# Sigmoid attention and a GELU feed-forward layer on one core: the first pair's scores from unsplit float32, values products between them, and weight decoding that begins in the fourth unit and goes on at one chunk a product in block 0

## The chip, the cores and the metric

The kernel runs on one core of a Trainium2 chip. A core has a matrix engine (TensorE, PE in the profile, with its weight loads as PEld), a vector engine (DVE), an activation engine (ACT), GpSimd (POOL), and a sync engine (SP) that here only issues DMAs. Each engine works through its own instructions in order and waits on semaphores for the others. The metric is the device time of one execution in microseconds (us); the median of three runs of the kernel before is 1192.38 us.

## The reference

Eight batches, twelve heads, 448 positions, head size 64; the 3584 tokens of 768 values that come out go through a feed-forward layer of width 2048.

```python
def _attn_ref(q, k, v):
    S = q.shape[2]
    scale = 1.0 / np.sqrt(q.shape[-1])
    scores = scale * np.matmul(q, k.transpose(0, 1, 3, 2)) - np.log(S)
    attn = 1.0 / (1.0 + np.exp(-scores))
    return np.matmul(attn, v).astype(np.float32)

def _moe_ref(x, w_in, w_out):
    h = x @ w_in
    g = 0.5 * h * (1.0 + erf(h * inv_sqrt2))
    return (g @ w_out).astype(np.float32)
# x: the attention output, as (batch * position) x (head * size)
```

The attention weights are a sigmoid of each score, so no row needs a maximum or a sum. `w_in` (768 x 2048) and `w_out` (2048 x 768) arrive as 64-bit floats. The host only lays data out; the kernel itself turns the 64-bit patterns into float32. That is the decoding of which the title speaks.

## The kernel before, in words

**Attention** runs over 24 units; a unit is one batch and four heads, held as two pairs p = 0, 1 of two heads each. For each pair, `scores` makes three chunks of 128 keys. A score is a sum of three products in a fast float32 format ("fp32r"), of a rounded part `hi` and a rest `lo` of q and k: lo·hi, hi·lo, hi·hi, two heads side by side in the array, 18 matmuls for a pair. `split` makes the parts: for pair 0, ACT rounds (L245) and DVE subtracts (L248); for pair 1, DVE does both (L247, L248). `scores_tail` does the last 64 keys of all four heads from the raw float32 data (L277). Each chunk goes through a sigmoid on ACT (L252) from one of three PSUM buffers (`ps_sc`), so a chunk's products wait until the sigmoid three chunks earlier is done. `values` (L298) and `values_tail` (L311) multiply the sigmoids by v in plain float32, one unit behind the scores; `park` copies the sums from PSUM (L324, DVE) and GpSimd writes them to a scratch `scr_x` in HBM.

**Decoding** is a list of steps, taken in program order by `dec.to(c)` up to c chunks. There are 40 chunks: 16 of `w_in` (768 columns each) and 24 half units of `w_out` (512 each). A chunk needs, on DVE, L99, L100 and L103 (`start`); on ACT, L110 and L113 (`scale`); then on DVE, L119 and L124 (`end`). A finished unit goes to HBM scratch through GpSimd's queue. The 64-bit data come in by SP (`raw`, three buffers), three loads ahead of the first chunk and then one at each `end`. Before the change, chunk 0 is decoded in unit 0, 20 chunks are done within attention (`AHEAD = 20`), ten more beside the sixteen w_in products of block 0, the last ten beside block 0's w_out products.

**Feed-forward** runs over seven blocks t of 512 tokens. `ffn1` makes 16 tiles of 128 hidden features, 18 matmuls each (lo·hi, hi·lo, hi·hi over six parts of 128, L370 to L372); ACT applies GELU twice (L375 `gf` in float32, L376 `g` rounded) and DVE subtracts (L377). `ffn2` makes six output tiles from two halves of 24 matmuls each (L398 to L400). All need the weights split as well. `Weights` streams each decoded unit from scratch (`wst`, three buffers), ACT rounds it (L184), DVE subtracts (L185), into one of four buffers `whl`. `W.get` of unit i first prepares every unit up to i + 3. Thus, in program order, unit i + 3's cast and subtraction come after tile i - 1's GELU, subtraction and decoding step, and before tile i's.

Nothing reorders this: the order on each engine is the order in which the program is written. At the end of the attention `load_x`, `split_x` and `W.prepare_to(2)` make the first block's inputs ready, and ACT loads its GELU table (L375) before the first `gf`.

Of the kernel before, what the change touches and what calls it, by code (L numbers as in the profile page):

```python
# [21 lines left out]
def tile_sigmoid_attention_gelu_ffn(  # L22
# [131 lines left out]
                self.taken += 1  # L154

    dec = Decoder()
    AHEAD = 20

    class Weights:
        def __init__(self):  # L160
# [48 lines left out]
    def attention(at, ps_sc, ps_av):  # L209
# [3 lines left out]
        def load(u):  # L213
            if u >= total:
                return
            b, n = divmod(u, NU)
            raw = at.tile([P, 2, 2, S], F32, tag="qk", name=f"qk{u}", bufs=3)
            pairs = (slice(0, 1), slice(1, 2)) if u == 0 else (slice(0, 2),)
            for ps in pairs:
                hps = slice(2 * n + ps.start, 2 * n + ps.stop)  # L220
                nc.sync.dma_start(raw[:, ps, 0], q[b, hps].rearrange("p r s -> r p s"))
                for j in range(2):
                    src = k[b, hps, rows(j), j].rearrange("p r s -> r p s")
                    nc.sync.dma_start(raw[rows(j), ps, 1], src)
            raws[u] = raw

        def load_v(u):
# [27 lines left out]
        def scores(u, p, c):  # L255
            if u >= total:
                return
            hi, lo = parts[u, p]
            sc = ps_sc.tile([P, 2, 512], F32, tag="sc", name=f"sc{u}_{p}_{c}")[:, :, :S]
            keys = slice(c * P, c * P + P)  # L260
            terms = ((hi, lo), (lo, hi), (hi, hi))
            for n, (ks, qs) in enumerate(terms):
                for j in range(2):
                    nc.tensor.matmul(  # L264
                        sc[:, j], ks[rows(j), 1, keys], qs[rows(j), 0], start=n == 0, stop=n == 2
                    )
            sigmoid(u, p, c, sc)

# [19 lines left out]
                pavs[u, p] = ps_av.tile([P, 512], F32, tag=f"pav{p}", name=f"pav{u}_{p}")  # L288
            return pavs[u, p][:, :S]

        def values(u, p):
            if u < 0:
                return
            pav = bank(u, p)
            for c in range(FULL):
                a = probs.pop((u, p, c))
                for j in range(2):
                    nc.tensor.matmul(  # L298
                        pav[rows(j)],
                        vals[u][:, p, j, c],  # L300
                        a[:, j],
                        start=p == 0 and c == 0,
                        stop=p == 1 and c == FULL - 1,
                    )
# [22 lines left out]
                nc.gpsimd.dma_start(scr_x[:, 2 * n : 2 * n + 2, b * S : (b + 1) * S], xs.pop(u))  # L327

        load(0)
        split(0, 0)  # L330
        split(0, 1)
        load(1)
        load_v(0)
        dec.to(-0.25)
        load_v(1)
        load(2)
        for u in range(total + 1):
            dec.to(min(u + 0.5, AHEAD) if u > 0 else 0)
            for c in range(FULL):
                scores(u, 0, c)  # L340
            values(u - 1, 0)
            split(u + 1, 0)
            split(u + 1, 1)
            for c in range(FULL):
                scores(u, 1, c)
            scores_tail(u)
            load(u + 3)
            values_tail(u - 1)
            dec.to(min(u + 1, AHEAD))
            park(u - 1, 0)  # L350
            values(u - 1, 1)
            park(u - 1, 1)
            load_v(u + 2)
            if u == total - 2:
                load_x(0)
                W.load_to(2)
            if u == total - 1:
                split_x()
                W.prepare_to(2)

    def feed_forward(ff, ps_f):
        def ffn1(t):
            g = []
            for fc in range(NF):
# [12 lines left out]
                nc.vector.tensor_tensor(gt[:, 1], gf, gt[:, 0], op=ALU.subtract)  # L377
                g.append(gt)
                if t == 0:
                    dec.to(AHEAD + 10 * (fc + 1) / NF)  # L380
            return g

        def ffn2(t, g):
            for e in range(NE):
                po = ps_f.tile([P, T], F32, tag="pf", name=f"po{t}_{e}")
                for half in range(2):
                    hl = W.get((t, "out", 2 * e + half))
                    if t == 0:
                        dec.to(AHEAD + 10 + 2 * e + half + 1)
                    if e == 1 and half == 0 and t + 1 < NT:  # L390
                        load_x(t + 1)
                    if e == 2 and half == 0 and t + 1 < NT:
                        split_x()
                    for f in range(NFH):
                        fc = half * NFH + f
                        wh = hl[:, 0, f * P : (f + 1) * P]
                        wl = hl[:, 1, f * P : (f + 1) * P]
                        nc.tensor.matmul(po, wl, g[fc][:, 0], start=fc == 0, stop=False)  # L398
                        nc.tensor.matmul(po, wh, g[fc][:, 1], start=False, stop=False)  # L399
                        nc.tensor.matmul(po, wh, g[fc][:, 0], start=False, stop=fc == NF - 1)  # L400
                ob = ff.tile([P, T], F32, tag="tmp", name=f"ob{t}_{e}", bufs=3)
                nc.scalar.copy(ob, po)  # L402
                nc.sync.dma_start(out[e * P : (e + 1) * P, t * T : (t + 1) * T], ob)

        for t in range(NT):
            ffn2(t, ffn1(t))

    nc.vector.memset(one, 1.0)
    nc.scalar.activation(one, one, AF.Sigmoid)
    with tc.tile_pool(name="at", bufs=1) as at:  # L410
        with psum("ps_sc", 3) as ps_sc, psum("ps_av", 1) as ps_av:
            attention(at, ps_sc, ps_av)
# [36 lines left out]
```

## Time and profile before

| | |
|---|---|
| Three runs, median (lowest to highest) | 1192.38 us (1191.7 to 1193.59) |
| The profiled execution's own time | 1189.64 us |
| Its span, first to last instruction | 1187.9 us |
| DVE busy, share of the span | 528.1 us, 44% |
| ACT busy, share of the span | 547.5 us, 46% |

The profiled execution is 1.74 us longer than its span, and 2.74 us shorter than the median of the runs. By stage, in us from the span's start (the stage of block 0's w_in products, 266.6 to 331.8, is quoted in the prediction):

| stage | length | PE busy | DVE busy | ACT busy | DMA share |
|---|---|---|---|---|---|
| 0 to 16.4, first unit | 16.4 | 8.81 | 6.85 | 10.04 | 0.84 |
| 16.4 to 27.5, second unit | 11.1 | 7.74 | 7.17 | 8.08 | 1.06 |
| 27.5 to 266.6, rest of attention | 239.1 | 239.10 | 153.16 | 179.27 | 0.83 |
| 331.8 to 397.2, block 0, w_out products | 65.4 | 62.88 | 46.69 | 30.43 | 0.71 |
| 397.2 to the end, blocks 1 to 6 | 790.7 | 787.08 | 262.42 | 279.56 | 0.36 |

PE busy counts overlapped matmuls once. Rows of the timeline, used below, give start and duration in us, the engine, the line and operation, what is written from what with sizes, how many instructions the row merges, and in brackets the idle time before the row and what ended it. A "chain" row gives start, length and what the end of the program goes back to.

### The profile page before, as it was taken

How to read it: one execution, taken by the hardware profiler on the slowest of the kernel's cores; microseconds unless marked ns; L12 is line 12 of the kernel's file. 1: busy time of each engine (PE TensorE's matmuls, PEld its weight loads, DVE VectorE, ACT ScalarE, POOL GpSimd, SP SyncE). 2: the span in 40 equal slices, each digit the busy share in tenths (PEclk: the TensorE clock that was granted, in tenths of full speed). 3: DMA queues.
4: the chain of work that ended last, by engine and by line, in shares of the span. 5: the costliest groups of instructions: out<-in, count | busy, mean ns of one | idle time of the engine just before them, and what ended most of it. 6: DMA issues, size and time to landing. Idle time of an engine off the chain costs nothing.

```text
span 1187.9 us, 14649 instructions
## 1 busy us (share of the span) xinstructions
PE 1170.8 (99%) x5856; PEld 884.8 (74%) x5856; DVE 528.1 (44%) x643; ACT 547.5 (46%) x751; POOL 36.0 (3%) x56
## 2 busy tenths in 40 slices
PE   6999999999999999999999999999999999999998
PEld 3554544548888788888888888888888888888887
DVE  4777776447878334323432243324432343323420
ACT  6777777666644344324432343324432443324420
POOL 0111111000000000000000000000000000000000
PEclk9999999999999999999999999999999999999999
DMA  9999988646767533523343333433343334433330
GB/s 304 304 286 295 293 281 257 203 159 214 237 244 262 182 94 124 181 81 109 118 171 98 107 111 115 155 119 94 120 159 111 102 106 169 120 98 98 120 115 27
DMA packets 71300, 194.42 MB, mean 164 GB/s; under 512 B 6976, under 2 KB 19648, under 8 KB 71232
## 3 DMA queue, kind: packets, MB, share of 16 engines
q1 hardware_dynamic: 65536, 169.89, 45.6%
q0 software_dynamic: 5696, 23.60, 4.9%
q8 instruction: 46, 0.75, 0.3%
q14 instruction: 22, 0.18, 0.0%
HBM read 158.86 MB, written 34.60 MB: 163 GB/s over the span
## 4 chain that ended last, share of the span: by engine, by line
PE 81%; issue 15%; DMA 2%; POOL 1%; SPq 0%; ACT 0%; DVE 0%; POOLq 0%; ACTq 0%
PE po L398 11%; PE po L399 11%; PE po L400 11%; PE ph L370 11%; PE ph L371 11%; PE ph L372 11%; PE pav L298 7%; PE sc L264 5%; DMA qk<-k_dram 1%; PE sc_t L277 1%; PE pav L311 1%; POOL scr_out L128 0%; POOL scr_x L327 0%; DMA wst<-scr_out 0%; DMA scr_out<-wd_out 0%
## 5 line engine op out<-in xcount | busy, mean ns | idle before, releaser
L185 DVE TENSOR_TENSOR whl<-wst,whl 128x768 fp32r<-128x768 f32 (+1 forms) x196 | 210.0, 1072 | 299.3 <-ACT whl L184 296.5
L398 PE MATMUL po<-g,whl 128*128 128x512 f32 x672 | 261.8, 390 | 2.5 <-DVE whl L185 2.4
L370 PE MATMUL ph<-xh,whl 128*128 128x512 f32 x672 | 261.5, 389 | 0.0
L400 PE MATMUL po<-g,whl 128*128 128x512 f32 x672 | 261.4, 389 | 0.0
L399 PE MATMUL po<-g,whl 128*128 128x512 f32 x672 | 261.4, 389 | 0.0
L372 PE MATMUL ph<-xh,whl 128*128 128x512 f32 x672 | 261.4, 389 | 0.0
L371 PE MATMUL ph<-xl,whl 128*128 128x512 f32 x672 | 261.4, 389 | 0.0
L184 ACT CAST whl<-wst 128x768 fp32r<-128x768 f32 (+1 forms) x196 | 181.7, 928 | 140.5 <-PE po L400 117.2
L377 DVE TENSOR_TENSOR g<-gf,g 128x512 fp32r<-128x512 f32 x112 | 77.4, 692 | 232.0 <-ACT g L376 231.9
L375 ACT ACTIVATE gf<-ph 128x512 f32<-128x512 f32 x112 | 67.0, 598 | 224.4 <-PE ph L372 196.9
L252 ACT ACTIVATE a<-sc 128x896 f32<-128x896 f32 x144 | 121.9, 919 | 59.9 <-PE sc L264 59.9
L398 PEld LDWEIGHTS po<-g,whl 128*128 128x128 f32 x672 | 126.1, 188 | 29.9 <-DVE whl L185 3.8
L370 PEld LDWEIGHTS ph<-xh,whl 128*128 128x128 f32 x672 | 126.1, 188 | 26.9 <-DVE whl L185 0.7
L372 PEld LDWEIGHTS ph<-xh,whl 128*128 128x128 f32 x672 | 126.1, 188 | 26.3
L400 PEld LDWEIGHTS po<-g,whl 128*128 128x128 f32 x672 | 126.1, 188 | 26.3
L399 PEld LDWEIGHTS po<-g,whl 128*128 128x128 f32 x672 | 126.1, 188 | 26.1
L371 PEld LDWEIGHTS ph<-xl,whl 128*128 128x128 f32 x672 | 126.1, 188 | 26.1
L298 PE MATMUL pav<-a,v 128*64 128x448 f32 x576 | 118.6, 547 | 0.0
L402 ACT COPY ob<-po 128x512 f32<-128x512 f32 x42 | 24.7, 587 | 172.5 <-PE po L400 170.9
L298 PEld LDWEIGHTS pav<-a,v 128*64 128x64 f32 x576 | 37.2, 136 | 69.7 <-issue 69.7
L376 ACT ACTIVATE g<-ph 128x512 fp32r<-128x512 f32 x112 | 66.4, 593 | 0.0
L264 PE MATMUL sc<-lo,hi 64*128 64x448 f32 x288 | 58.4, 402 | 6.8 <-DVE lo L248 6.8
(35 smaller groups left out, 666.5 us busy)
## 6 DMA issues: line engine op xcount, KB each, us to landing
wst<-scr_in SPq DMA_DIRECT2D x112, 384.0 KB, 3.2
wst<-scr_out SPq DMA_DIRECT2D x84, 512.0 KB, 3.4
v<-v_dram SPq DMA_DIRECT2D x24, 512.0 KB, 5.2
raw<-w_in_dram SPq DMA_DIRECT2D x16, 768.0 KB, 8.0
raw<-w_out_dram SPq DMA_DIRECT2D x24, 512.0 KB, 5.1
scr_x<-x POOLq DMA_DIRECT2D x24, 448.0 KB, 6.8
xl<-scr_x SPq DMA_DIRECT2D x7, 1536.0 KB, 8.0
out_dram<-ob SPq DMA_DIRECT2D x42, 256.0 KB, 2.1
```

The lines of the kernel that those rows point to most:

```text
L184: nc.scalar.copy(hl[:, 0, :w], t[:, :w])
L185: nc.vector.tensor_tensor(hl[:, 1, :w], t[:, :w], hl[:, 0, :w], op=ALU.subtract)
L252: nc.scalar.activation(a, sc, AF.Sigmoid, bias=NEG_LOG_S, scale=SCALE)
L264: nc.tensor.matmul(sc[:, j], ks[rows(j), 1, keys], qs[rows(j), 0], start=n == 0, stop=n == 2)
L298: nc.tensor.matmul(pav[rows(j)], vals[u][:, p, j, c], a[:, j], start=p == 0 and c == 0, stop=p == 1 and c == FULL - 1,)
L370: nc.tensor.matmul(ph, wl, xh[:, cc], start=cc == 0, stop=False)
L371: nc.tensor.matmul(ph, wh, xl[:, cc], start=False, stop=False)
L372: nc.tensor.matmul(ph, wh, xh[:, cc], start=False, stop=cc == NC - 1)
L377: nc.vector.tensor_tensor(gt[:, 1], gf, gt[:, 0], op=ALU.subtract)
L398: nc.tensor.matmul(po, wl, g[fc][:, 0], start=fc == 0, stop=False)
L399: nc.tensor.matmul(po, wh, g[fc][:, 1], start=False, stop=False)
L400: nc.tensor.matmul(po, wh, g[fc][:, 0], start=False, stop=fc == NF - 1)
```

## The change

- **Start.** The first pair of unit 0 is no longer split: its three chunks are one product each from the raw float32 data. Its two k transfers are issued from ACT's queue, where all others stay on SP's. `load_v(0)` moves ahead of `load(1)`. The dummy sigmoid that makes ACT load its table moves behind ACT's two transfers.
- **Values.** Unit 0's pair-0 values products are written between the pair-1 score chunks of unit 0, no longer in unit 1.
- **Decoding in attention** begins in the fourth unit (`BEGIN = 3`); its first three loads are issued at the start of the third. 21 chunks are done in attention.
- **Decoding in block 0** goes at one chunk for each of the sixteen w_in tiles (before: ten in sixteen); three are left for the w_out products.
- **End.** The very last output tile is copied from PSUM in two halves, one by ACT and one by DVE, and stored by two transfers.

```diff
-    AHEAD = 20
+    AHEAD, BEGIN = 21, 3
...
+                first = u == 0 and ps.start == 0
...
-                    nc.sync.dma_start(raw[rows(j), ps, 1], src)
+                    (nc.scalar if first else nc.sync).dma_start(raw[rows(j), ps, 1], src)
...
-            terms = ((hi, lo), (lo, hi), (hi, hi))
+            if (u, p) in parts:
+                hi, lo = parts[u, p]
+                terms = ((hi, lo), (lo, hi), (hi, hi))
+            else:
+                terms = ((raws[u][:, p],) * 2,)
...
         load(0)
-        split(0, 0)
+        nc.scalar.activation(one, one, AF.Sigmoid)
         split(0, 1)
+        load_v(0)
         load(1)
-        load_v(0)
-        dec.to(-0.25)
         load_v(1)
         load(2)
         for u in range(total + 1):
-            dec.to(min(u + 0.5, AHEAD) if u > 0 else 0)
+            if u == BEGIN - 1:
+                dec.to(-0.25)
+            dec.to(min(u + 0.5 - BEGIN, AHEAD) if u >= BEGIN else -1)
             for c in range(FULL):
                 scores(u, 0, c)
-            values(u - 1, 0)
+            if u != 1:
+                values(u - 1, 0)
             split(u + 1, 0)
             split(u + 1, 1)
             for c in range(FULL):
                 scores(u, 1, c)
+                if u == 0:
+                    values(0, 0, (c,))
...
-            dec.to(min(u + 1, AHEAD))
+            dec.to(min(u + 1 - BEGIN, AHEAD) if u >= BEGIN else -1)
...
                 if t == 0:
-                    dec.to(AHEAD + 10 * (fc + 1) / NF)
+                    dec.to(AHEAD + fc + 1)
...
                     if t == 0:
-                        dec.to(AHEAD + 10 + 2 * e + half + 1)
+                        dec.to(AHEAD + NF + 2 * e + half + 1)
...
-                nc.scalar.copy(ob, po)
-                nc.sync.dma_start(out[e * P : (e + 1) * P, t * T : (t + 1) * T], ob)
+                dst = out[e * P : (e + 1) * P, t * T : (t + 1) * T]
+                if (t, e) == (NT - 1, NE - 1):
+                    for h, copy, queue in (
+                        (slice(0, T // 2), nc.scalar.copy, nc.scalar),
+                        (slice(T // 2, T), nc.vector.tensor_copy, nc.sync),
+                    ):
+                        copy(ob[:, h], po[:, h])
+                        queue.dma_start(dst[:, h], ob[:, h])
+                else:
+                    nc.scalar.copy(ob, po)
+                    nc.sync.dma_start(dst, ob)
```

What stands on the engines now is seen at two places. The first is ACT in block 0, from the GELUs of the first tile on. A `g_` row ends a tile, `me` is a decoding buffer, `whl` a split weight buffer. Before:

```order
L376 ACTIVATE g_0_2707<-ph_0_2678 128x512
L110 ACTIVATE me_2717<-me_2717 128x512
L113 ACTIVATE me_2717<-me_2717 128x512
L184 CAST whl_2724<-wst_2682 128x768
L375 ACTIVATE gf_1_2748<-ph_1_2723 128x512
L376 ACTIVATE g_1_2747<-ph_1_2723 128x512
L184 CAST whl_2762<-wst_2687 128x768
L375 ACTIVATE gf_2_2786<-ph_2_2761 128x512
L376 ACTIVATE g_2_2785<-ph_2_2761 128x512
L110 ACTIVATE me_2757<-me_2757 128x512
L113 ACTIVATE me_2757<-me_2757 128x512
L184 CAST whl_2793<-wst_2727 128x768
```

And of the change, at the same place:

```order
L389 ACTIVATE g_0_2702<-ph_0_2673 128x512
L110 ACTIVATE me_2712<-me_2712 128x512
L113 ACTIVATE me_2712<-me_2712 128x512
L184 CAST whl_2719<-wst_2677 128x768
L388 ACTIVATE gf_1_2743<-ph_1_2718 128x512
L389 ACTIVATE g_1_2742<-ph_1_2718 128x512
L110 ACTIVATE me_2752<-me_2752 128x512
L113 ACTIVATE me_2752<-me_2752 128x512
L184 CAST whl_2759<-wst_2682 128x768
L388 ACTIVATE gf_2_2783<-ph_2_2758 128x512
L389 ACTIVATE g_2_2782<-ph_2_2758 128x512
L110 ACTIVATE me_2792<-me_2792 128x512
```

Before, the pair L110, L113 stood ahead of the next weight cast L184 in some tiles only; now it stands there in every tile, through the sixteenth. On DVE at that place, a tile of the change reads as follows (L390 is the subtraction that was L377):

```order
L390 TENSOR_TENSOR g_0_2702<-gf_0_2703,g_0_2702 128x512
L119 SCALAR_TENSOR_TENSOR me_2539<-raw_2326,me_2539 128x512
L124 SCALAR_TENSOR_TENSOR wd_out_2708<-me_2539 128x512
L99 TENSOR_SCALAR me_2712<-raw_2430 128x512
L100 TENSOR_SCALAR me_2712<-raw_2430 128x512
L103 SCALAR_TENSOR_TENSOR me_2712<-raw_2430,me_2712 128x512
L185 TENSOR_TENSOR whl_2719<-wst_2677,whl_2719 128x768
L390 TENSOR_TENSOR g_1_2742<-gf_1_2743,g_1_2742 128x512
```

These eight rows repeat for each of the sixteen tiles, where before some tiles had only the first and the last two of them. The second place is SP's queue from the start of the program. Before:

```order
L224 DMA qk_82<-k_dram 64x448 x2
L221 DMA qk_97<-q_dram 128x2x448
L224 DMA qk_97<-k_dram 64x2x448 x2
L233 DMA v_101<-v_dram 128x2x512
L91 DMA raw_103<-w_in_dram 128x768
L91 DMA raw_105<-w_in_dram 128x768
L91 DMA raw_107<-w_in_dram 128x768
L233 DMA v_109<-v_dram 128x2x512
L221 DMA qk_111<-q_dram 128x2x448
```

And of the change (`qk_81` is unit 0, `qk_95` unit 1, `qk_101` unit 2):

```order
L225 DMA qk_81<-k_dram 64x448 x2
L234 DMA v_93<-v_dram 128x2x512
L222 DMA qk_95<-q_dram 128x2x448
L225 DMA qk_95<-k_dram 64x2x448 x2
L234 DMA v_99<-v_dram 128x2x512
L222 DMA qk_101<-q_dram 128x2x448
L225 DMA qk_101<-k_dram 64x2x448 x2
L222 DMA qk_169<-q_dram 128x2x448
```

The three loads of raw weights between unit 1's and unit 2's data are gone from here; they stand behind unit 4's data now. Unit 0's v stands ahead of unit 1's q and k.

More of the change, by code (lines that the diff above doesn't have):

```diff
@@ L257, in scores @@
                 return
-            hi, lo = parts[u, p]
             sc = ps_sc.tile([P, 2, 512], F32, tag="sc", name=f"sc{u}_{p}_{c}")[:, :, :S]
             keys = slice(c * P, c * P + P)
-            terms = ((hi, lo), (lo, hi), (hi, hi))
+            if (u, p) in parts:
[3 more added lines that the diff above has]
+                terms = ((raws[u][:, p],) * 2,)
+            last = len(terms) - 1
             for n, (ks, qs) in enumerate(terms):
@@ L264, in scores @@
                     nc.tensor.matmul(
-                        sc[:, j], ks[rows(j), 1, keys], qs[rows(j), 0], start=n == 0, stop=n == 2
+                        sc[:, j],
+                        ks[rows(j), 1, keys],
+                        qs[rows(j), 0],
+                        start=n == 0,
+                        stop=n == last,
                     )
@@ L289, in bank, with values @@
             return pavs[u, p][:, :S]
-        def values(u, p):
+        def values(u, p, chunks=range(FULL)):
             if u < 0:
@@ L294, in values @@
             pav = bank(u, p)
-            for c in range(FULL):
+            for c in chunks:
                 a = probs.pop((u, p, c))
@@ L408, in tile_sigmoid_attention_gelu_ffn @@
     nc.vector.memset(one, 1.0)
-    nc.scalar.activation(one, one, AF.Sigmoid)
     with tc.tile_pool(name="at", bufs=1) as at:
```

## The prediction

> **What bounds the kernel now.** I read the page's first part, then the waits, then busy time by stage, then the timeline at the places where PE waits.
>
> ```profile
> span 1187.9 us, 14649 instructions
> PE 1170.8 (99%) x5856; PEld 884.8 (74%) x5856; DVE 528.1 (44%) x643; ACT 547.5 (46%) x751; POOL 36.0 (3%) x56
> ```
> ```profile
> PE sc L264 <- DVE lo L248: 6.8, 1, 6.8
> PE sc_t L277 <- ACT a L252: 4.1, 2, 3.4
> PE po L398 <- DVE whl L185: 2.4, 2, 1.7
> ```
>
> The matrix engine bounds the program. It waits at three places only: 6.8 us before its first product, 4.1 us in the second unit, 2.4 us in block 0's w_out products. So a change can win some 13 us here and little more, apart from half-rate time; and it loses wherever PE begins to wait. DVE and ACT look idle on average. The average is misleading for block 0:
>
> ```profile
> 266.60:331.80 65.20, 65.20 (x289) 53.98 (x288) 51.79 (x83) 40.15 (x65) 3.44 (x6) 1.00 0.70 232
> ```
>
> These are the sixteen w_in tiles (stage, length, then busy time of PE, PEld, DVE, ACT, POOL). PE never waits and takes 65.20 / 16 = 4.08 us a tile. DVE is busy for 51.79 of 65.20 us with ten chunks. The change puts sixteen there.
>
> **Block 0, the term that decides.** Here is one tile with a whole chunk, on DVE and on ACT.
>
> ```profile
> 276.29 0.69 DVE L377 TENSOR_TENSOR g<-gf,g 128x512 fp32r<-128x512 f32 x1 [5.37 <-ACT g L376]
> 276.90 0.68 DVE L119 SCALAR_TENSOR_TENSOR me<-raw,me 128x512 uint32<-128x512 uint32 x1
> 277.62 0.69 DVE L124 SCALAR_TENSOR_TENSOR wd_out<-me 128x512 f32<-128x512 uint32 x1
> 278.23 0.42 DVE L99 TENSOR_SCALAR me<-raw 128x512 uint32<-128x512 uint32 x1
> ...
> 280.74 0.96 DVE L185 TENSOR_TENSOR whl<-wst,whl 128x768 fp32r<-128x768 f32 x1 [1.02 <-ACT whl L184]
> 281.72 0.69 DVE L377 TENSOR_TENSOR g<-gf,g 128x512 fp32r<-128x512 f32 x1
> ```
> ```profile
> 278.68 0.63 ACT L110 ACTIVATE me<-me 128x512 f32<-128x512 int32 x1 [2.43 <-DVE me L99]
> 279.35 0.63 ACT L113 ACTIVATE me<-me 128x512 uint32<-128x512 f32 x1
> 279.88 0.82 ACT L184 CAST whl<-wst 128x768 fp32r<-128x768 f32 x1
> 280.61 0.59 ACT L375 ACTIVATE gf<-ph 128x512 f32<-128x512 f32 x1
> 281.10 0.59 ACT L376 ACTIVATE g<-ph 128x512 fp32r<-128x512 f32 x1
> ```
>
> This is a ring through both engines, each strictly in its order. L377, L119, L124 and L99 on DVE take 2.36 us to the moment (278.65) at which ACT's L110 may start; ACT's L110, L113 and weight cast L184 follow, up to 280.70; DVE's L185 waits for that cast, and the next L377 comes behind L185 (and behind ACT's GELUs). From L377 to L377: 281.72 - 276.29 = **5.43 us**, against PE's 4.08. It is no accident of the first tile:
>
> ```profile
> 304.85 0.69 DVE L377 TENSOR_TENSOR g<-gf,g 128x512 fp32r<-128x512 f32 x1
> ...
> 310.27 0.69 DVE L377 TENSOR_TENSOR g<-gf,g 128x512 fp32r<-128x512 f32 x1
> ```
> ```profile
> 291.60 0.68 DVE L377 TENSOR_TENSOR g<-gf,g 128x512 fp32r<-128x512 f32 x1
> ...
> 295.80 0.68 DVE L377 TENSOR_TENSOR g<-gf,g 128x512 fp32r<-128x512 f32 x1
> ```
>
> 5.42 us again; but 4.20 us in another tile with a chunk, in which ACT's cast had been done ahead of that chunk's L110. Before the change the tiles were mixed (also some without a chunk, 1.5 us), and the mean stayed under PE's pace. In the new order L110 and L113 stand ahead of L184 in each of sixteen tiles, so I take 5.43 for each, with 4.20 as the lower end.
>
> PE feels it through the weights. Unit m's L185 stands behind the chunk of tile m - 4, so unit m is ready 5.41 us after L377 of that tile: at 276.29 + 5.43 (m - 4) + 5.41. On its own, PE would start tile m at 266.63 + 4.08 m. Tile 5: ready at 287.1, wanted at 287.0. From there PE follows the ring: tile 15 is ready at 341.4, wanted at 327.8. The next weights are 1024 wide:
>
> ```profile
> L185 DVE TENSOR_TENSOR whl<-wst,whl 128x1024 fp32r<-128x1024 f32 x84 | 102.9, 1225 | 201.1 <-ACT whl L184 200.3 <-PE po L400 0.8
> L184 ACT CAST whl<-wst 128x1024 fp32r<-128x1024 f32 x84 | 88.3, 1051 | 87.9 <-PE po L400 77.0 <-DMA wst<-scr_out 10.9
> ```
>
> 1.23 against 0.96 and 1.05 against 0.82 us, so the last three turns take 5.43 + 0.27 + 0.23 less some overlap, 5.8. The last L377 starts at 276.29 + 12 x 5.43 + 3 x 5.8 = 358.9 and ends at 359.5. The first w_out tile's second half needs it for its last three products (0.7 us), and ends at 360.2. Unhindered, it ends at 266.63 + 65.20 + 2 x 5.44 = 342.7 (a half is 24/18 of 4.08). **Cost: +17.5 us.** Behind that, a w_out half without L377 turns in 341.82 - 336.62 = 5.20 us by the rows below, under PE's 5.44, with three chunks left; nothing more is lost.
>
> ```profile
> 336.62 0.69 DVE L119 SCALAR_TENSOR_TENSOR me<-raw,me 128x512 uint32<-128x512 uint32 x1
> ...
> 341.82 0.68 DVE L119 SCALAR_TENSOR_TENSOR me<-raw,me 128x512 uint32<-128x512 uint32 x1
> ```
>
> The ring starts when ACT gets to its first GELU, held by a table load at 273.88, just as the last transfer to `scr_x`, issued by POOL at 268.24, has landed. I keep that; 3 us earlier or later moves the cost as much, 14.5 to 20.5. In return, with decoding nearly done, the 2.4 us wait for w_out weights goes (**-2.4**, at worst 0).
>
> **Start.** These rows, of ACT's timeline and of the chain that ended last, show the old one.
>
> ```profile
> 4.70 0.94 ACT L245 CAST hi<-qk 128x896 fp32r<-128x896 f32 x1 [2.47 <-DMA qk<-k_dram]
> ...
> 12.22 2.54 ACT L252 ACTIVATE a<-sc 128x896 f32<-128x896 f32 x3
> ```
> ```profile
> 1.19 0.56 SPq L224
> ...
> 1.80 0.58 SPq L224
> ...
> 5.52 4.97 DMA qk<-k_dram
> ...
> 10.51 11.94 DMA qk<-k_dram
> ...
> 22.47 0.94 ACT hi L245
> ...
> 24.27 1.77 PE sc_t L277 x8
> ...
> 27.54 2.41 PE pav L298 x12
> 29.95 2.04 PE sc L264 x18
> ...
> 36.41 0.92 PE sc_t L277 x8
> ...
> 40.48 2.02 PE sc L264 x18
> ```
>
> Unit 2's data, behind three raw loads, land at 10.51 + 11.94 = 22.45; ACT's rounding and a sigmoid hold PE until 24.27, and the stretch from there to unit 2's scores takes 29.95 - 24.27 = 5.68 us where the same stretch of the next unit takes 40.48 - 36.41 = 4.07: 1.61 us lost to a halved clock (sc_t 1.77 against 0.92 us). I measure the gain at that sc_t.
>
> After the change the first products need no splitting: they start at about 4.1 (the pair landed at 4.7; of the two k issues on SP, 0.56 and 0.58 us, a second queue saves one), 2.7 us before the old first product at 6.8. Six plain products take 2.41 us (L298) where a pair's 18 split ones take 2.04, so the new form costs 0.4 us of PE at full rate, twice that cold. But PE then waits for ACT, so the sum runs along ACT. Unit 1's q and k landed at 5.52 + 4.97 = 10.49; now unit 0's v stands ahead (128 x 2 x 512 floats, 0.52 MB, 1.7 us at the 307 GB/s of a stage quoted below) while SP's issues come 1.2 us sooner, without the two: 11.0. From there ACT has unit 1's cast, three sigmoids of unit 0 pair 1, its tail, three of unit 1, unit 2's cast, and one more sigmoid, whose PSUM buffer the sc_t needs: eight sigmoids at 0.84 (2.54 / 3) and two casts at 0.94 make 8.6, and sc_t starts at 19.6. Unit 2's data need 1.44 MB (v of unit 1, then q and k) behind 11.0, 4.7 us, and are there in time at 15.7; the raw loads come later, under units with slack. **Gain: 24.27 - 19.6 + 1.6 = 6.3 us.** No long idle time should be left to halve the clock; if PE warms up 3 us later, or data come 1 us later, the gain is 4.5; at the earliest 7.
>
> **Rest.** In attention, units 3 to 23 each carry one chunk, as units 0 to 19 did, under 10.5 us of PE each: nothing. The last chunk's L110 and L113 now stand ahead of the first block's rounding on ACT, 1.2 us, but DVE is free for it only when the last sums are parked, so it is covered. The interleaved values are the same products elsewhere: nothing. The end: DVE's half copy stands behind ACT's in the order of waits, two short copies and a half transfer in place of one copy and a whole one: 0, between -0.2 and +0.3.
>
> **Sum** against the profiled execution: 1189.64 - 6.3 + 17.5 - 2.4 + 0 = 1198.4, +8.8 us. The runs' median stands 2.74 above that execution; 1192.38 + 8.8 = **1201.2**. The ends together: -7 + 14.5 - 2.4 - 0.2 = +4.9 and -4.5 + 20.5 + 0 + 0.3 = +16.3.
>
> **Rivals.** (a) The ring doesn't bind: ACT gets its casts done ahead, tiles turn in 4.20 us, and the sum above gives 276.29 + 12 x 4.2 + 3 x 4.6 + 1.4 = 341.9, under 342.7. Then only gains stand, -8.7: **1183.7**, faster. It decides below 4.25 us a turn. For it: the 4.20 us tile, and DVE's mere 79% in that stage. Against: the written order in every tile; 7 in 100. (b) A turn of about 4.9 us, were part of ACT's work to overlap: 276.29 + 12 x 4.9 + 3 x 5.3 + 1.4 = 352.4, a cost of 9.7 and **1193.4**; 7 in 100. (c) The start doesn't gain, because ACT's queue issues late or PE stays cold: **1206 to 1207.5**, 5 in 100. (d) The clock. The stretch below is the only one with a reduced clock (0.85), behind a 3.36 us idle time; the 0.77 us gap at 13.19 left a tail at full rate, 1.08 us.
>
> ```profile
> 16.40:27.50 11.10, 7.74 (x50) 3.20 (x48) 7.17 (x9) 8.08 (x11) 0.75 (x1) 0.85 1.06 307
> 13.19 1.08 PE L277 MATMUL sc_t<-qk 64*64 64x448 f32 x8 [0.77 <-ACT a L252]
> ```
>
> Block 0 would now have 1.35 us gaps in ten tiles. If these halved the clock for half of them, a tile would take 8.2 in place of 5.43, 5 x 2.7 = 14 us: **1215**, 5 in 100. The Trainium skill, "TensorE: Matmul & The Clock Gate", section "A second HAM failure mode: psum-queue depth-cycling", speaks for this: where PE idles briefly but often between groups of matmuls, its clock swings between half and full. The same page's section "Why this matters for your kernels" warns only of idle gaps over about 3 us; by that rule there is no loss here, and the trace agrees so far, with the halving behind 3.36 us and none behind 0.77.
>
> **How the numbers follow.** The forecast has 76 in 100, (a) 7, (b) 7, (c) 5, (d) 5. The range, 1195 to 1207, holds the forecast's bounds but for their last 2 us, and most of (c); (a), (d) and most of (b) are left out. A measurement of this kernel can tell about 0.2%, 2.4 us. Faster by more: (a) and a little of (b), 0.08. Within: most of (b), 0.07. Slower: 0.85.
>
> **What would show it.** In the changed profile: L390 at 5.4 us steps through block 0's sixteen tiles, and PE waiting for `whl` L185 by some 17 us; the stage of w_in tiles near 80 us in place of 65; no PE wait in the w_out tiles; unit 1's sc_t near 19.6; PE's first product near 4. Steps near 4.2 there would prove me wrong, and the kernel would be faster.

## The result, and the profile after

| | before | changed |
|---|---|---|
| median (lowest to highest), six runs each | 1192.13 us (1190.73 to 1193.59) | 1199.94 us (1198.95 to 1201.0) |
| profiled execution | 1189.64 us | 1199.94 us |
| its span | 1187.9 us | 1198.2 us |

The changed kernel is slower: ratio of the times 1.0066, 95% interval 1.0053 to 1.0079, or +7.8 us at the medians (predicted: +8.8, 1201.2 us).

Here are the engines' line of the changed kernel's page and its waits of PE (engine, line, what it waited for; us in total, times, longest):

```profile
PE 1175.2 (98%) x5850; PEld 883.8 (74%) x5850; DVE 528.0 (44%) x643; ACT 545.9 (46%) x750; POOL 36.1 (3%) x56
```
```profile
PE ph L383 <- DVE whl L185: 10.8, 11, 1.1
PE sc L269 <- DMA qk<-k_dram: 4.6, 1, 4.6
PE po L411 <- DVE whl L185: 1.5, 1, 1.5
PE sc_t L286 <- ACT a L253: 1.2, 2, 0.8
PE po L411 <- ACT g L389: 0.5, 1, 0.5
PE po L412 <- DVE g L390: 0.4, 1, 0.4
```

A new wait leads, mostly about 1 us each time, for the split weights in block 0's w_in tiles. DVE and ACT are as idle on average as before, with the same busy time; neither average gives this away. The stage's row does (stage, length, then busy time of PE, PEld, DVE, ACT, POOL):

```profile
262.20:343.46 81.26, 68.99 (x290) 53.12 (x288) 59.58 (x97) 42.08 (x69) 3.98 (x7) 1.00 0.67 208
```

81.26 us where it was 65.4, with DVE busy for 73% of it. (The 65.4 runs from block 0's first w_in product to its first w_out product in the trace of before.) PE reads 68.99 and not 65.4 because the profile's matmul ends are modelled: each of twelve gaps, the eleven of the first row above and the one of the third, hides some 0.3 us, so the waits view (10.8 + 1.5) gives less than the loss of 15.9. Here is DVE's timeline, and ACT's, at the second tile:

```profile
272.37 0.69 DVE L390 TENSOR_TENSOR g<-gf,g 128x512 fp32r<-128x512 f32 x1 [5.93 <-ACT g L389]
...
276.82 0.96 DVE L185 TENSOR_TENSOR whl<-wst,whl 128x768 fp32r<-128x768 f32 x1 [1.03 <-ACT whl L184]
277.80 0.69 DVE L390 TENSOR_TENSOR g<-gf,g 128x512 fp32r<-128x512 f32 x1
...
283.23 0.69 DVE L390 TENSOR_TENSOR g<-gf,g 128x512 fp32r<-128x512 f32 x1
```
```profile
274.76 0.64 ACT L110 ACTIVATE me<-me 128x512 f32<-128x512 int32 x1 [2.42 <-DVE me L99]
...
275.97 0.82 ACT L184 CAST whl<-wst 128x768 fp32r<-128x768 f32 x1
```

L390 comes every 5.43 us; I call one such round through both engines a turn. In each turn ACT stands 2.42 us for DVE, and DVE 1.03 us for ACT: both wait, so neither is full. The start, from PE's timeline and the chain that ended last:

```profile
4.61 4.39 PE L269 MATMUL sc<-qk 64*128 64x448 f32 x10 [4.61 <-DMA qk<-k_dram]
...
21.39 0.98 PE L286 MATMUL sc_t<-qk 64*64 64x448 f32 x8 [0.77 <-ACT a L253]
...
25.46 0.47 PE L269 MATMUL sc<-lo,hi 64*128 64x448 f32 x2
```
```profile
5.28 7.74 DMA qk<-k_dram
...
13.09 0.94 ACT hi L246
14.03 4.23 ACT a L253 x6
...
21.39 0.98 PE sc_t L286 x8
```

Unit 1's data land at 5.28 + 7.74 = 13.02, ACT takes over, and unit 2's first scores start at 25.46, where the trace of before has 29.88.

**Three marks** carry the rest: the start of unit 2's first scores, of block 0's first product, and the end of PE's last matmul, from each kernel's timeline, one trace each. Columns in us.

| kernel | to unit 2's scores | to block 0's first product | to PE's last end | rest | span |
|---|---|---|---|---|---|
| before | 29.88 | 236.75 | 917.65 | 3.59 | 1187.9 |
| changed | 25.46 | 236.73 | 931.97 | 3.98 | 1198.2 |
| e1, old pace | 25.29 | 236.76 | 914.21 | 4.00 | 1180.3 |
| e2, new pace alone | 31.88 | 236.73 | 932.01 | 3.59 | 1204.2 |
| e3, half a step | 25.30 | 236.73 | 914.21 | 4.00 | 1180.2 |
| r1, cast ahead | 25.03 | 236.73 | 938.03 | 4.02 | 1203.8 |
| h1, k on SP | 27.29 | 236.73 | 931.83 | 4.01 | 1199.9 |
| h4, late begin, 21 chunks | 25.31 | 236.72 | 914.21 | 3.60 | 1179.9 |
| h5, 20 chunks | 27.01 | 236.73 | 917.77 | 4.00 | 1185.5 |
| h6, first pair split | 26.31 | 236.73 | 915.78 | 3.99 | 1182.8 |
| h7, rounding later | 24.43 | 236.72 | 914.47 | 3.61 | 1179.2 |
| h8, h4 and plain pair | 26.06 | 236.72 | 914.21 | 3.61 | 1180.6 |
| b1, before again | 31.98 | 236.73 | 918.93 | 3.60 | 1191.2 |
| b2, before again | 33.54 | 236.73 | 917.81 | 3.60 | 1191.7 |

The second column never moves: attention behind unit 2 is the same work at full rate everywhere. The third shows what block 0 loses, for blocks 1 to 6 have no wait of PE: 914.21 in four kernels, though 914.47 in h7, where the view shows no wait either, so a few tenths can't be read from it. The first varies from one execution to the next.

### The profile page after: what moved, and what is told of

It is laid out like the page before. It is cut to its first block, busy times and chain, and to the rows that moved or that the text cites. A ratio compares the mean times of both kernels' runs of the same rounds, so it can differ in the third digit from the quotient of the medians.

```text
span 1198.2 us, 14643 instructions
## 1 busy us (share of the span) xinstructions
PE 1175.2 (98%) x5850; PEld 883.8 (74%) x5850; DVE 528.0 (44%) x643; ACT 545.9 (46%) x750; POOL 36.1 (3%) x56
## 4 chain that ended last, share of the span: by engine, by line
PE 92%; DVE 3%; ACT 3%; DMA 1%; issue 0%; SPq 0%; ACTq 0%; DVEq 0%
PE po L412 12%; PE po L413 12%; PE po L411 12%; PE ph L383 12%; PE ph L384 12%; PE ph L385 12%; PE pav L307 9%; PE sc L269 7%; PE sc_t L286 2%; DVE whl L185 1%; PE pav L320 1%; DMA qk<-k_dram 1%; ACT a L253 1%; ACT whl L184 1%; ACT me L113 0%
## 5 line engine op out<-in xcount | busy, mean ns | idle before, releaser
L185 DVE TENSOR_TENSOR whl<-wst,whl 128x768 fp32r<-128x768 f32 (+1 forms) x196 | 210.0, 1073 | 320.0 <-ACT whl L184 310.8
L383 PE MATMUL ph<-xh,whl 128*128 128x512 f32 x672 | 262.9, 391 | 10.8 <-DVE whl L185 10.8
L184 ACT CAST whl<-wst 128x768 fp32r<-128x768 f32 (+1 forms) x196 | 181.6, 927 | 129.3 <-PE po L413 125.2
L390 DVE TENSOR_TENSOR g<-gf,g 128x512 fp32r<-128x512 f32 x112 | 77.5, 692 | 230.9 <-ACT g L389 230.7
L389 ACT ACTIVATE g<-ph 128x512 fp32r<-128x512 f32 x112 | 66.3, 592 | 0.0
L249 DVE TENSOR_TENSOR lo<-qk,hi 128x896 fp32r<-128x896 f32 x47 | 51.5, 1096 | 18.4 <-ACT hi L246 17.3
```

Source lines behind the costliest of these rows:

```text
L184: nc.scalar.copy(hl[:, 0, :w], t[:, :w])
L185: nc.vector.tensor_tensor(hl[:, 1, :w], t[:, :w], hl[:, 0, :w], op=ALU.subtract)
L383: nc.tensor.matmul(ph, wl, xh[:, cc], start=cc == 0, stop=False)
```

## The experiments

The theory: block 0's ring of waits costs some 17 us, and the start gives some back. The rivals: the amount of decoding work costs the time, or its late begin, or the new start.

### Block 0: pace, work, or order

**e1.** The changed kernel with the old pace.

```diff
-                    dec.to(AHEAD + fc + 1)
+                    dec.to(AHEAD + 10 * (fc + 1) / NF)
-                        dec.to(AHEAD + NF + 2 * e + half + 1)
+                        dec.to(AHEAD + 10 + 2 * e + half + 1)
```

> The changed kernel with block 0's old pace (ten chunks beside the sixteen w_in tiles, two a w_out half behind them); all else of the change stays. Theory R (the ring L390, L119, L124, L99, L110, L113, L184, L185 of 5.43 us a tile costs the time): the ring is gone from most tiles, PE no longer waits some 14 us for whl L185 beside w_in, up to 2.5 us of the wait in the w_out tiles come back, and the time falls from 1199.9 by 14 (between 12 and 17) to about 1186 (1183 to 1188). Rival H (part of the 16.8 us lies elsewhere, in the later start of decoding or in the head): it falls by less than 10 us, to above 1190. The start's gain of 4.4 us, read at unit 2's first scores (25.5 in place of 29.95), should stay as it is.

Measured: 1182.04 us (four runs, 1180.97 to 1182.63), ratio to before 0.9912 (0.9899 to 0.9926). That is 17.9 us below the changed kernel, more than expected, since the w_out wait did not come back. All the waits that PE has left, and the stage's row:

```profile
PE sc L269 <- DMA qk<-k_dram: 4.4, 1, 4.4
PE sc_t L286 <- ACT a L253: 1.4, 2, 0.8
```
```profile
262.05:327.46 65.41, 65.41 (x290) 54.16 (x289) 51.87 (x84) 40.27 (x65) 3.36 (x6) 1.00 0.70 224
```

**e2.** The reverse: the kernel before with those two lines of the change, AHEAD still 20.

```diff
-                    dec.to(AHEAD + 10 * (fc + 1) / NF)
+                    dec.to(AHEAD + fc + 1)
-                        dec.to(AHEAD + 10 + 2 * e + half + 1)
+                        dec.to(AHEAD + NF + 2 * e + half + 1)
```

> The kernel before with the new pace of block 0 alone (one whole chunk a tile); AHEAD stays at 20 and nothing of the head or the end is changed. Theory R: the ring costs 16.8 and the removed wait of the w_out weights gives back 2.4, so the time rises from 1192.1 by 14 to about 1206.5 (1204 to 1209), and L377 comes at steps of 5.43 us. Rival H (the later start of decoding is needed for the loss): less than 5 us of rise, below 1197.

Measured: 1204.92 us (four runs, 1204.37 to 1205.98), ratio 1.0106 (1.0093 to 1.012), +12.8. The pace alone makes the loss; neither the late begin nor the new start is needed. Its trace shows the changed kernel's waits in block 0 nearly number for number; the two leading ones are:

```profile
PE ph L370 <- DVE whl L185: 10.9, 11, 1.1
...
PE po L398 <- DVE whl L185: 1.5, 1, 1.5
```

**e3.** The changed kernel, sixteen chunks beside sixteen tiles as there, but half a step earlier.

```diff
-                    dec.to(AHEAD + fc + 1)
+                    dec.to(AHEAD + fc + 0.5)
```

> The changed kernel with sixteen chunks beside the w_in tiles as now, each shifted by half a step: a tile has L110 and L113 of one chunk and then L119, L124 and L99, L100, L103 of the next, so that L110 finds its operand ready from the tile before. The same instructions, the same DVE and ACT busy time. Theory R (the chain of waits within a tile, not the amount of work): steps fall from 5.43 to 4.1 to 4.4 us (DVE's own work of a tile, 5.43 less its wait of 1.03, is 4.40), the cost from 16.8 to between 0 and 3, and the time to 1183 to 1187, below the kernel before. Rival D (sixteen chunks are too much work for DVE and ACT in whatever order): steps stay at 5.2 or more and the time above 1197.

Measured: 1182.33 us (five runs, 1181.7 to 1182.61), ratio 0.9915 (0.9902 to 0.9929): level with e1, and 17.6 us below the changed kernel, from half a step. The stage's row, then DVE's and ACT's timelines:

```profile
262.03:327.44 65.41, 65.41 (x290) 54.16 (x289) 57.85 (x98) 44.04 (x71) 3.99 (x7) 1.00 0.78 256
```
```profile
279.47 0.95 DVE L185 TENSOR_TENSOR whl<-wst,whl 128x768 fp32r<-128x768 f32 x1
280.34 0.68 DVE L390 TENSOR_TENSOR g<-gf,g 128x512 fp32r<-128x512 f32 x1
...
283.67 0.95 DVE L185 TENSOR_TENSOR whl<-wst,whl 128x768 fp32r<-128x768 f32 x1
```
```profile
278.52 0.64 ACT L110 ACTIVATE me<-me 128x512 f32<-128x512 int32 x1 [1.20 <-DVE me L99]
...
279.73 0.82 ACT L184 CAST whl<-wst 128x768 fp32r<-128x768 f32 x1
280.45 0.59 ACT L388 ACTIVATE gf<-ph 128x512 f32<-128x512 f32 x1
280.94 0.59 ACT L389 ACTIVATE g<-ph 128x512 fp32r<-128x512 f32 x1
```

Turns of 4.20 us (L185 to L185), with not one idle time of DVE in them. The reason I wrote down holds in part. L110 does take what L99 wrote one tile before, but it does not find it ready: it waits 1.20 us. What that order allows is that ACT gets a tile ahead. DVE's L185 at 279.47 starts before ACT's L184 at 279.73, and L390 at 280.34 before L389 at 280.94: DVE takes what ACT made a turn earlier. One engine runs a step behind the other, so only ACT waits. DVE was busy 57.85 us in 65.41 here, against 59.58 in 81.26 in the changed kernel: the work was never too much.

**r1.** The changed kernel with the next weight's cast and subtraction ahead of the chunk.

```diff
                 if t == 0:
+                    W.prepare_to(fc + 1 + WHL)
                     dec.to(AHEAD + fc + 1)
```

> The changed kernel with its new pace, and in each of block 0's w_in tiles the next weight's cast L184 and subtraction L185 taken ahead of the chunk (L184 right behind the GELUs, ahead of L110; L185 right behind L390, ahead of L119). My prediction's second rival named this order as what would make a turn 4.20 us. Theory R, summed from the changed kernel's rows: the chunk's L110 and L113 still stand between L99 and the next tile's GELUs, which L390 waits for, so the ring only changes its links: 1.73 (L390, wait for L184, L185) + 0.72 + 0.61 + 0.45 + 0.67 + 0.54 + 0.49 + 0.62 = 5.83 us a turn, no less than 5.43, and the time is 1200 to 1207. Rival N (the late cast alone is what binds): turns of 4.2 to 4.5 us, PE's wait for whl gone, and 1182 to 1187.

Measured: 1206.07 us (four runs, 1205.58 to 1206.56), ratio 1.0115 (1.0098 to 1.0132), 6.1 us slower still. DVE's timeline:

```profile
277.02 0.69 DVE L390 TENSOR_TENSOR g<-gf,g 128x512 fp32r<-128x512 f32 x1 [1.27 <-ACT g L389]
277.75 0.96 DVE L185 TENSOR_TENSOR whl<-wst,whl 128x768 fp32r<-128x768 f32 x1
...
282.71 0.69 DVE L390 TENSOR_TENSOR g<-gf,g 128x512 fp32r<-128x512 f32 x1 [1.27 <-ACT g L389]
```

The turn is 282.71 - 277.02 = 5.69 us (summed: 5.83). DVE's wait has only moved, from L185 to L390, 1.27 us. So an early cast alone does not open the ring. What does is the step of distance between the engines, as in e3. The last GELU also comes later, and PE, done with what it had, waits for it in one piece; PE's waits, and PE's windows around that place (the number behind POOL is the granted clock):

```profile
PE po L412 <- ACT g L389: 4.7, 1, 4.7
```
```profile
353.00:357.20 4.20, 0.35 (x2) 0.00 (x0) 3.69 (x6) 1.44 (x3) 0.00 (x0) 1.00 0.85 270
357.20:364.00 6.80, 5.96 (x13) 4.42 (x14) 5.33 (x9) 2.99 (x5) 0.54 (x1) 0.51 0.58 198
```

6.8 us at half rate follow, 3.4 us of r1's extra 6.06.

### The w_out wait

**h5.** e1 with 20 chunks done by the end of attention.

```diff
-    AHEAD, BEGIN = 21, 3
+    AHEAD, BEGIN = 20, 3
```

> The changed kernel with block 0's old pace and with 20 chunks in place of 21 done by the end of attention. Theory A (the one chunk more, not the later begin, took the wait of the w_out weights away): the stretch from block 0's first product to the last one goes back from 914.2 to 917.6 us, with PE waiting 2.5 us for whl L185 in block 0's w_out tiles as in the kernel before, and the time rises from 1182.0 by 3.4 to 1185.5. Rival: the wait was settled by how late the decoding begins; it stays away and the time stays within 1 us of 1182.0.

Measured: 1185.47 us (four runs, 1184.9 to 1187.28), ratio 0.9944 (0.9929 to 0.9958), +3.4 on e1 (the profiled run is the slowest of the four). The wait is back, and the third mark is 917.77, as before:

```profile
PE po L411 <- DVE whl L185: 2.6, 3, 1.3
```

One chunk more in attention removes that wait. The faster pace was not needed for it, though e2 shows that the pace does it too: with 20 chunks, its third mark (932.01) is that of the changed kernel with 21.

### The start

**h1.** The changed kernel with the first pair's k on SP's queue.

```diff
-                    (nc.scalar if first else nc.sync).dma_start(raw[rows(j), ps, 1], src)
+                    nc.sync.dma_start(raw[rows(j), ps, 1], src)
```

> The changed kernel with the first pair's k on SP's queue again, as before the change; all else as changed. Read at three places: PE's first product (4.61), the landing of unit 1's second k (13.02), unit 2's first scores (25.53). Theory Q (unit 1's data came 2.0 us later than I reckoned because two queues share the transfer engines and a k issue stood waiting): the first product comes 0.6 to 1.2 us later, unit 1's data land at 12.0 or before, and unit 2's scores come earlier by up to 1 us. Rival V (v of unit 0, moved ahead of unit 1's q and k, is what delays them): they land at 12.8 to 13.5 as now, and unit 2's scores stay within 0.3 us.

One run, 1201.64 us. The first product came earlier, at 4.14, where I expected it later; unit 1's last k landed at 14.85, and unit 2's scores started 1.83 us later. Both theories miss. Taking the second queue away did not bring unit 1's data sooner, and I can't tell from one trace whether the rest is h1's edit or the spread of the landings (below). What the place of unit 0's v costs stays open.

**h4.** The kernel before with the late begin and with 21 chunks in place of 20, and nothing else.

```diff
-    AHEAD = 20
+    AHEAD, BEGIN = 21, 3
...
-        dec.to(-0.25)
...
-            dec.to(min(u + 0.5, AHEAD) if u > 0 else 0)
+            if u == BEGIN - 1:
+                dec.to(-0.25)
+            dec.to(min(u + 0.5 - BEGIN, AHEAD) if u >= BEGIN else -1)
...
-            dec.to(min(u + 1, AHEAD))
+            dec.to(min(u + 1 - BEGIN, AHEAD) if u >= BEGIN else -1)
```

> The kernel before with decoding begun in the fourth unit (BEGIN 3, AHEAD 21) and nothing else: first pair split as before, values not interleaved, k on SP's queue, block 0's old pace, old end. Theory B (the start's gain comes from the three raw loads alone, which stood ahead of unit 2's data and held PE for 3.4 to 4.8 us): the first product stays at 6.8 to 7.4, unit 1's sc_t comes at 20.9 to 22 without that wait, unit 2's first scores at 25.0 to 26.0 (25.5 in the changed kernel), the w_out wait is gone with the one chunk more that is done before block 0, and the time is 1181 to 1183, level with the run with the old pace (1182.0). Rival P (plain float32 and interleaved values, with a first product 2.2 us earlier, carry 2 us or more of the gain): unit 2's scores come at 27.5 or later and the time is 1184 or more.

Measured: **1181.5 us** (five runs, 1181.33 to 1181.65), ratio 0.9907 (0.9893 to 0.9922). Its first product comes 2.6 us later than the changed kernel's, its unit 2 scores at the same time (25.31 and 25.46). PE's only wait behind its first product:

```profile
PE sc_t L277 <- ACT a L252: 0.7, 1, 0.7
```

The long wait at unit 2's data is gone (its last k lands at 18.90, where it landed at 22.45 behind the raw loads), and with it the start's whole gain is there. The w_out wait is gone too, as h5 has it, by the 21st chunk.

**h8.** h4, and in it the first pair in plain float32.

```diff
-            terms = ((hi, lo), (lo, hi), (hi, hi))
+            if (u, p) in parts:
+                hi, lo = parts[u, p]
+                terms = ((hi, lo), (lo, hi), (hi, hi))
+            else:
+                terms = ((raws[u][:, p],) * 2,)
...
-        split(0, 0)
```

> The run with the later begin of decoding alone (1181.5), and in it the first pair's scores in plain float32; values not interleaved, k on SP's queue, v of unit 0 behind unit 1's q and k, as before the change. Theory B (behind the first product PE and ACT are held in turn by unit 1's data, which land at 11.6 to 13, and by their own work): the first product comes 2.5 to 3 us earlier, at 4.1 to 4.7, and unit 2's first scores at 24.3 to 25.3, at most 1 us earlier than 25.3; the time is 1180.3 to 1181.8. Rival P: the earlier start is carried through, unit 2's scores come at 22.3 to 23.5, and the time is 1178.5 to 1179.7.

Measured: 1182.54 us (four runs, 1181.06 to 1183.51), ratio 0.9916 (0.9901 to 0.993). First product at 3.99, unit 2's scores at 26.06: 3.2 us earlier at the one end, 0.75 later at the other. Neither theory said later; unit 1's last k landed at 12.51, in h4 at 11.60. PE's only wait behind the first product shows where the earlier start went:

```profile
PE sc_t L281 <- ACT a L252: 2.5, 1, 2.5
```

PE runs dry at unit 0's tail and waits 2.5 us, for a sigmoid that stands on ACT behind unit 1's rounding, which waits for unit 1's data.

**h6.** e1 with the first pair split again.

```diff
         nc.scalar.activation(one, one, AF.Sigmoid)
+        split(0, 0)
```

> The changed kernel with block 0's old pace and with the first pair split again (18 products in place of 6 plain ones); k stays on ACT's queue, values stay interleaved. Theory B (PE has work without a pause from its first product to unit 1's sc_t, so a later first product is paid in full, less what the plain form costs): the first product comes at 7.5 to 8, 3.2 us later than 4.4, and unit 2's scores move by 1 to 2.5 us, from 25.3 to between 26.3 and 27.8; the time is 1183 to 1184.5. Rival C (ACT and unit 1's data at 12.9 bind there, as my sum had it): unit 2's scores stay within 0.5 us of 25.3 and the time within 0.6 of 1182.0.

Measured: 1184.2 us (four runs, 1183.5 to 1184.61), ratio 0.993 (0.9916 to 0.9944), +2.2 on e1. The first product moved by 3.3 us, unit 2's scores by 1.0; 1.6 us of the profiled run lie in one w_out wait, seen in no other kernel with 21 chunks and the old pace. Theory B's ranges hold, the time only with that wait, which it did not have. By these two traces the plain form is worth about 1 us where values are interleaved, and by h4 and h8 nothing; but unit 1's last k landed 1.4 us earlier in h6 than in e1, and 0.9 later in h8 than in h4, so neither is shown.

**h7.** e1 with unit 1's rounding behind the second pair-1 score of unit 0, and one copy and one store at the end.

```diff
-            split(u + 1, 0)
-            split(u + 1, 1)
+            if u > 0:
+                split(u + 1, 0)
+                split(u + 1, 1)
             for c in range(FULL):
                 scores(u, 1, c)
                 if u == 0:
                     values(0, 0, (c,))
+                if u == 0 and c == 1:
+                    split(1, 0)
+                    split(1, 1)
...
```

> The changed kernel with block 0's old pace, with unit 1's rounding put behind the second of unit 0's pair 1 scores (ACT stood 2.5 us at that rounding, waiting for unit 1's data, with two sigmoids ready behind it), and with one copy and one store at the end as before. Theory C (ACT's order makes the two waits of PE at sc_t, 0.6 and 0.8 us): both waits go, unit 2's scores come 0.6 to 1.4 us earlier, at 23.9 to 24.7; with 0.4 from the end (PE's last product to the end of the span 3.6 in place of 4.0) the time is 1180.2 to 1181.0. Rival: unit 1's scores, now behind a later rounding, take the time back; unit 2's scores stay at 25.3 or later, and only the end's 0.4 is left, 1181.6.

Measured: 1182.04 us (five runs, 1181.03 to 1182.41), ratio 0.9912 (0.9897 to 0.9926): the same median as e1, later than either theory said. In the trace the start is 0.86 us earlier, the wait at unit 0's tail is gone, and the rest behind PE's last matmul is 3.61 in place of 4.00. The end is clear, as in every kernel with the single copy; whether the 0.86 holds from run to run is open.

### The trace of before

**b1, b2.** The kernel before, unchanged, twice.

> The kernel before, unchanged, for a second trace of it: its profiled execution (1189.64) lay 2.5 us below its median, and my sum took that distance as one that the change leaves alone. Theory S (the distance lies in the wait of unit 2's sc_t behind the raw loads, which the change removes; the run with the new pace alone showed unit 2's first scores at 31.88 in place of 29.88): the time is near 1192, unit 2's scores come at 31 to 33, and from there everything is as in the first trace, 236.7 us to block 0's first product and 917.7 from there to the last product. Rival: the 2.5 us lie spread over the later stages; unit 2's scores come within 0.5 us of 29.9, and the 917.7 grow by 1.5 or more.

> The same kernel once more, with the same two readings: by theory S unit 2's first scores move with the time of the execution, one for one, and the later stages don't; by the rival the later stages move.

Measured: 1193.01 and 1193.44 us. Rows of PE's timeline of b1 and of b2 at unit 1's tail, and each one's windows from 20 to 34 us:

```profile
26.45 1.77 PE L277 MATMUL sc_t<-qk 64*64 64x448 f32 x8 [5.31 <-ACT a L252]
```
```profile
26.55 1.77 PE L277 MATMUL sc_t<-qk 64*64 64x448 f32 x8 [4.92 <-ACT a L252]
```
```profile
20.00:34.00 14.00, 8.69 (x58) 3.90 (x54) 6.66 (x10) 6.97 (x9) 1.33 (x2) 0.88 1.05 269
```
```profile
20.00:34.00 14.00, 9.08 (x50) 3.55 (x48) 5.63 (x9) 6.34 (x8) 0.75 (x1) 0.76 1.05 280
```

PE waits 5.31 and 4.92 us where the first trace had 3.36, and the half clock behind that lasts about 3.4 us in b1 (0.12 of 14 us, doubled) and 6.7 in b2. Unit 2's scores come at 31.98 and 33.54; with e2, which has the same start, 31.88. The first trace, 29.88, had drawn a short wait. The later stretch moves too, by 1.3 us in b1 and 0.2 in b2, so theory S holds for most of the distance.

## Why the prediction was right, and where it was not

| term | predicted | by the marks | shown by |
|---|---|---|---|
| ring in block 0 | +17.5 | 931.97 - 914.21 = +17.8 | e1, e2, e3 |
| wait for w_out weights | -2.4 | 914.21 - 917.65 = -3.4 | e1, h5 |
| start, against the first trace | -6.3 | 25.46 - 29.88 = -4.4 | h4 |
| start, against e2, b1 and b2 | | -6.4 to -8.1 | b1, b2 |
| end | 0 | +0.4 | h4, h7, h8 |
| sum | +8.8 | +10.3 (spans of the two traces); +7.8 at the medians | |

**The ring** was right in mechanism and size: 5.43 us a turn in twelve turns, then three of 5.8, PE waiting from the sixth tile on, a stage of 81.26 us where I had said near 80. PE does wait in the w_out tiles (1.5, 0.5 and 0.4 us), which my list of signs denied; they are the ring's end, the last two of them for the last GELU and its subtraction, as my own sum had it. Rival (a) named the right bound, 4.20 us, and e3 reaches it. Its reading of the 4.20 us tile was right, but it missed what makes that tile short. These are ACT's rows there, and DVE's:

```profile
291.22 0.82 ACT L184 CAST whl<-wst 128x768 fp32r<-128x768 f32 x1
...
292.43 0.59 ACT L376 ACTIVATE g<-ph 128x512 fp32r<-128x512 f32 x1
293.99 0.63 ACT L110 ACTIVATE me<-me 128x512 f32<-128x512 int32 x1 [0.96 <-DVE me L99]
...
295.19 0.82 ACT L184 CAST whl<-wst 128x768 fp32r<-128x768 f32 x1
```
```profile
294.93 0.95 DVE L185 TENSOR_TENSOR whl<-wst,whl 128x768 fp32r<-128x768 f32 x1
```

The cast at 291.22 is indeed ahead of L110, but r1 puts every cast there and turns in 5.69. In this tile the next GELU (292.43) stands ahead of L110 as well, and L185 starts before the cast behind it: it is e3's distance. It comes from the program: at ten chunks in sixteen tiles, `dec.to` often ends a tile between a chunk's `start` (L99) and its `scale` (L110). The two turns of 5.43 and 5.42 us quoted in the prediction are of tiles that take a whole chunk, and the new pace gives a whole chunk to every tile.

**The w_out wait** was mis-sized: I took the total of the waits view, and modelled matmul ends hide some 0.3 us in each of three gaps (0.11, 0.73 and 1.68 us before). From block 0's first w_out product to block 1's first product it is 68.71 us before and 65.28 in e1. (The stage given for it ahead of the prediction, to 397.2, ends too early: block 1 begins at 400.76.) The cause is not the pace alone, as I had it. The wait goes with the 21st chunk in attention (h5), so it is a gain that needs nothing of the new pace.

**The start** was mis-sized by two steps. "11.0": unit 1's data landed at 13.02 in the changed trace. I had let SP's issues come 1.2 us sooner, but v's issue now stands among them, and the last k is issued at 5.28 where it was 5.52, 0.24 us sooner. The rest is in the landings, which spread far more than the issues (last section). ACT's part behind it was right, 8.6 predicted and 8.3 measured (13.09 to 21.39). "The sum runs along ACT": it does so only while those data are late. In r1 they landed at 11.39, near my figure, and yet sc_t came at 20.96 and not at 11.39 + 8.6 = 20.0. This is r1's chain:

```profile
4.22 5.61 PE sc L269 x14
...
14.91 0.98 PE sc_t L286 x8
...
20.96 0.98 PE sc_t L286 x8
```

There PE itself has work without a gap from 4.22 to unit 0's tail at 14.91, with the plain products at half rate among it (ten in 4.39 us in the changed trace, where twelve values products of as many columns take 2.41). So the two engines share that path, and in this trace the early landing did not bring the gain to 6.3 against the first trace: unit 2's scores start at 25.03, 4.9 us earlier.

The credit went to the wrong part as well. The first product is indeed 2.2 us earlier, but h4, without it, gains as much: what counts is the three raw loads out of unit 2's way, and with them the half clock.

**From trace to median**: "The runs' median stands 2.74 above that execution" was added as if the change left that distance alone. Most of it lay in the very wait that the change removes. The four traces of the old start have their middle at 31.93, which makes the gain 6.5; from the medians, with the other terms taken off, it is 17.8 - 3.4 + 0.4 - 7.8 = 7.0. So my 6.3 is near the truth by errors that cancel, which is luck, and the total is +7.8 where the two traces give +10.3.

**The end** cost 0.4, just above my upper bound of 0.3: DVE's half copy waits for ACT's, so two short copies run one behind the other. The two stand in ACT's and DVE's timelines of the changed kernel:

```profile
1194.25 0.37 ACT L421 COPY ob<-po 128x256 f32<-128x256 f32 x1 [10.33 <-PE po L413]
1194.65 0.35 ACTq L422 DMA_DIRECT2D out_dram<-ob  x1
1194.65 0.42 DVE L421 COPY ob<-po 128x256 f32<-128x256 f32 x1 [19.42 <-ACT ob L421]
1195.11 0.33 SPq L422 DMA_DIRECT2D out_dram<-ob  x1
```

The last issue now starts 0.86 us behind the copy's start; with the single copy it is 0.61 us (1184.36 to 1184.97 before). That makes 0.25 of the 0.4; where the rest lies is not shown.

**The clock** (rival d) fell: the granted clock is 1.00 through the stage with its twelve gaps. The Trainium skill, "TensorE: Matmul & The Clock Gate", section "A second HAM failure mode: psum-queue depth-cycling", tells of a kernel whose clock swung behind brief, frequent idle times; this trace shows none of it, with gaps of 0.4 us, ten times 1.0 to 1.1 and 1.5, one in each turn. The same page's section "Why this matters for your kernels", which warns of gaps over about 3 us, agrees with every trace here: 3.36, 4.69, 4.81, 4.92 and 5.31 us halved the clock, 2.03 (h5) and 2.47 (h8) did not.

**The better kernel.** h4 takes the two parts that pay, the late begin and the 21st chunk, and leaves out the rest: 1181.5 us, 11 below the kernel before and 18 below the changed one. The new pace can stay if it is shifted by half a step (e3).

## What to carry to other kernels

Two engines that hand work to and fro within one step cost the sum of the chain (5.43 us a turn here), however idle both look; put one of them a step behind the other, and the same work costs only the busier one's time (4.20). Follow the in-order queues around the loop, add up one turn, and compare it with the bound engine's step before looking at busy shares. When a single trace stands apart from the median, look for the stage that varies, and ask whether the change touches just that stage.

## What the hardware showed that I had not expected

- **Half clock in steps.** Behind one idle time of PE, the clock was halved for about 3.4 us (before, behind 3.36 us; e2, behind 4.81; b1, behind 5.31) or about 6.8 (b2, behind 4.92; r1, behind 4.69): not in proportion to the idle time.
- **Landing times vary much more than engine times.** Unit 1's last k landed at 10.49 to 12.51 us in six traces with one order of transfers (before, e2, b1, b2, h4, h8), and at 11.39 to 14.56 in seven with the changed order (changed, e1, e3, h5, h6, h7, r1), while the 236.7 us behind unit 2's first scores repeat to 0.04. In e1 and h5, whose programs are the same that far, it landed at 12.84 and 14.56.
- **A second queue did not bring the first pair sooner.** With k on ACT's queue, in parallel to SP, the first product started at 4.22 to 4.61 us in six kernels (changed, e1, e3, r1, h5, h7); with all on SP at 4.14 (h1) and 3.99 (h8).
